# Four attention layers on one core: transfers queued by expected readiness, VectorE in source order, and the later weights' casts on POOL

## The chip, the core and the metric

The kernel runs on one core of a Trainium2 chip. The metric is the device time of one execution in microseconds. The engines are PE (matrix products), ACT (ScalarE), DVE (VectorE), POOL (GpSimd) and SP, whose queue issues all transfers of this kernel. Each engine takes its instructions strictly in the order of its own queue; an instruction whose operand is not there holds everything behind it on that engine.

## The reference

```python
# x: 2048 x 512, 32 heads of 16; layers A, B, A, B, each with wqkv (512 x 1536) and wo (512 x 512)
def layer(x, wqkv, wo, window):
    h = (x - mean(x)) / sqrt(var(x) + 1e-5)
    q, k, v = heads(h @ wqkv)
    scores = q @ k.T * 16 ** -0.5
    if window:                       # layers A: 0 <= query - key < 256
        scores = where(mask, scores, -1e9)
    return x + merge(softmax(scores) @ v) @ wo
```

Layers 0 and 2 are windowed (A), layers 1 and 3 are full (B).

## The kernel before, in words

Rows are handled in four chunks of 512 and heads in eight groups of four ("qd"). For a chunk and a group the attention makes transposed scores (keys on partitions, 512 queries free) in PSUM on PE (L673), ACT takes the exponential of two heads at a time out of PSUM (L677, tile `e`), in windowed layers POOL zeroes the edges of the window in `e` (L739 and L742), and PE multiplies `e` with the values, to which a column of ones is joined, into an accumulator `acc` (L717 full, L749 windowed), two steps later than the scores. Score banks come from a PSUM pool with three buffers; two accumulators stay. A full layer has 16 steps of two exponentials for each group, a windowed layer three steps.

Between the steps "side work" is issued: the output product of the chunk before (`wo`), the normalisation and transposes of the next layer (`T`), its keys, queries and values, and in layer 0 the preparation of weights that are needed later. A small planner in Python sets the order: a running clock in microseconds, `clock[0]`, is advanced by assumed costs, and each work has a time at which it is ready. A step of a windowed layer takes at least 2.4 units of that clock, a step of a full layer at least 1.8. PE takes its instructions in this source order (`manual_schedule`). For the other engines and for SP a scheduler chooses the order when the program is built, from priorities in source order and its own idea of when operands will be there; `high_priority` moves the copy `oe` ahead.

Steps that the change touches:

- `epilogue` (L609 to L650), at the end of a group: DVE copies the accumulator to `oe` (L617); SP sends its sums to `lt` (L622) and all of it to scratch DRAM `scr` (L623). After each second group `reciprocals` reads `lt`, takes reciprocals on DVE (L630 to L633), sends them to DRAM as `rcp` (L635), and loads `o` (L640) and the broadcast reciprocals `r` (L641). `normalised` multiplies `o` by `r` on DVE (L644) and splits the result into two f16 parts `oh` (L646, L647). `late` holds the two steps back by 4.5 and 8 units of the clock.
- `project` (L456): twelve f16 products make a bank of keys or queries (L387); the first part goes out through ACT (L479) or, in full layers, DVE (L481), the remainder through DVE (L482), the squares through ACT (L485) or POOL (L487), and SP stores both parts (L492 to L496). `queries` and `key_shift` add a row `m`.
- `wo` (L575) and `wo_part` (L592): DVE scales the output product to `dx` (L586, L604), adds it to `x` (L587, L605), SP stores `x` (L588, L606), and `stats` and `norm` (L402 to L417) prepare the next layer's normalised rows `xh`.
- `prep` (L338) prepares five of the eight weights during layer 0: `maxima` (L284) takes the largest absolute value over the four row blocks in one DVE instruction, `scales` makes scales from it, and `parts` (L319) multiplies by them on POOL (L326), casts to f16 on DVE (L332) and takes the remainder on POOL (L333).
- `load_full` (L686) and `load_win` (L698) load the next group's queries `qt` (two buffers) and keys `kt` (three buffers) a group ahead; `weights` (L367) loads a prepared weight into one of two buffers.

Of the kernel before, what the change touches and what calls it, by code (L numbers as in the profile page):

```python
# [19 lines left out]
P = 128  # L20
# [168 lines left out]
def fast_path(ctx, tc, flag, a_x, a_wqkv, a_wo, b_wqkv, b_wo, out):  # L189
# [12 lines left out]
    ctx.enter_context(tc.manual_schedule(engines={mybir.EngineType.PE}))  # L202
# [5 lines left out]
    CM, DN, WT, ST, LN, pend = {}, {}, {}, {}, {}, []  # L208

    clock, DONE, ONR = [0.0], {}, {}  # L210

    def spent(us):
        clock[0] += us
        return us
# [60 lines left out]
    def maxima(ty, s, raw, ahead):  # L275

        n = f"{ty}_{s}"
        if s == 3:
            for k in range(NC):
                nc.vector.tensor_scalar(raw[:, k, :], raw[:, k, :], upv[:, ty, k:k + 1], None, op0=ALU.mult)  # L280
        cm = CM[ty, s] = vp.tile([P, NHT], F32, name=f"wc{n}", tag="wc", bufs=8)
        if ahead:
            am = vp.tile([P, D], F32, name=f"wa{n}", tag="o")
            nc.vector.tensor_reduce(am, raw.rearrange("p k f -> p f k"), axis=AX.X, op=ALU.max,  # L284
                                    apply_absolute_value=True)
            yield
            pt = bank(f"wt{n}").rearrange("p (t f) -> p t f", f=P)
            for t in range(NHT):
                nc.tensor.transpose(pt[:, t, :], am[:, t * P:(t + 1) * P], ident)
            nc.vector.tensor_reduce(cm, pt, axis=AX.X, op=ALU.max)  # L290
            return
        for t in range(NHT):
            pt = bank(f"wt{n}_{t}")
            for k in range(NC):
                nc.tensor.transpose(pt[:, k * P:(k + 1) * P], raw[:, k, t * P:(t + 1) * P], ident)
            nc.vector.tensor_reduce(cm[:, t:t + 1], pt, axis=AX.X, op=ALU.max, apply_absolute_value=True)

    def scales(ty, s):

        n = f"{ty}_{s}"  # L300
        cm = CM.pop((ty, s))
# [4 lines left out]
        for v, name in ((up, "u"), (dn, "d"))[0 if s == 3 else 1:]:  # L306
            dg = vp.tile([P, NHT, P], F32, name=f"{name}g{n}", tag="oe")
            nc.vector.tensor_tensor(dg, ident[:, None, :].broadcast_to([P, NHT, P]),
                                    v[:, :, None].broadcast_to([P, NHT, P]), ALU.mult)
            yield  # L310
            pb = bank(f"{name}b{n}")
            nc.tensor.matmul(pb, onesf, dg.rearrange("p t f -> p (t f)"), start=True, stop=True)
            if name == "u":
                nc.vector.tensor_copy(gcol[ty], pb)
            else:
                DN[ty, s] = vp.tile([P, D], F32, name=f"wd{n}", tag="dn", bufs=2)
                nc.scalar.activation(DN[ty, s], pb, AF.Copy)

    def parts(ty, s, raw, act):  # L319

        dnb = DN.pop((ty, s))
        w = wp.tile([P, NC, 2, D], F16, name=f"w{ty}_{s}", tag="vf", bufs=NQ)
        for k in range(NC + 1):
            if k < NC:
                r = raw[:, k, :]
                (nc.vector if act else nc.gpsimd).tensor_tensor(r, r, dnb, ALU.mult)  # L326
            if k:
                r, (hi, lo) = raw[:, k - 1, :], (w[:, k - 1, b, :] for b in range(2))
                if act:
                    nc.scalar.activation(hi, r, AF.Copy)  # L330
                else:
                    nc.vector.tensor_copy(hi, r)  # L332
# [34 lines left out]
    def weights(ty, s, n, t=None):  # L367

        w = wp.tile([P, NC, 2, D], F16, name=f"w{n}", tag="w", bufs=WB)
        if t is None:  # L370
            nc.sync.dma_start(w, wd[ty, s])
            return w
        nc.sync.dma_start(w[:, :, :, :P], wd[ty, s][:, :, :, t * P:(t + 1) * P])
# [46 lines left out]
    def load_x(l, c):  # L420
        xs = []
        for i in range(4):
            k = 4 * c + i
            x = vp.tile([P, D], F32, name=f"x{l}_{k}", tag="x", bufs=XB)
            nc.sync.dma_start(x, a_x[0, k * P:(k + 1) * P, :] if l == 0 else xd[k])
            xs.append(x)
# [29 lines left out]
    def project(l, s, c, act, w=None, ht=None):  # L456
# [3 lines left out]
        if not w:  # L460
            w = weights(ty, s, n, ht)
            yield wait(8)
        xc = XC[l, c]
# [7 lines left out]
        for t in range(NHT) if ht is None else (ht,):  # L471
# [3 lines left out]
            settle(not sqs)  # L475
            sp = vp.tile([P, 2, QC], F16, name=f"sp{n}_{t}", tag="sp", bufs=3)
# [7 lines left out]
            if act:  # L484
                nc.scalar.activation(sq, ps, AF.Square, scale=e)  # L485
# [4 lines left out]
            d = dst[8 * t:8 * t + 8].rearrange("h (d b) n -> (h d) b n", b=4)  # L490
            if s:
# [30 lines left out]
    def queries(l, c, act, w=None, ht=None):  # L522
        sqs = yield from project(l, 0, c, act, w, ht)

        def rest():
            ph = squares(f"q{l}_{c}_{ht}", sqs)

            m = vp.tile([P, QC], F16, name=f"m{l}_{c}_{ht}", tag="m", bufs=1)
# [7 lines left out]
            for t in sqs:  # L536
                nc.sync.dma_start(rows(qs[l % 2, c])[8 * t:8 * t + 8, 3, :], m[32 * t:32 * t + 8, :])
# [6 lines left out]
    def key_shift(l, ht=None):  # L544
# [4 lines left out]
        nc.vector.tensor_reduce(kx[r], KM[l][r], axis=AX.X, op=ALU.max)  # L549
        m = vp.tile([P, QC], F16, name=f"mk{l}_{ht}", tag="m", bufs=1)  # L550
        nc.vector.tensor_scalar(m[r], ones[r], kx[r], -0.515, op0=ALU.mult, op1=ALU.mult)
        for t in range(NHT) if ht is None else (ht,):
            nc.sync.dma_start(rows(kf)[8 * t:8 * t + 8, 7, :].rearrange("h (c n) -> h c n", n=QC),
                              m[32 * t:32 * t + 8, None, :].broadcast_to([8, NQ, QC]))

    def values(l, c, act, w=None):
        n = f"{l}_{c}"
        if not w:
            w = weights(l % 2, 2, f"v{n}")
            yield wait(8)  # L560
        xc = XC[l, c]
# [13 lines left out]
    def wo(l, c):  # L575

        w = weights(l % 2, 3, f"o{l}_{c}")
        yield wait(8)

        xs = load_x(l, c)  # L580
        for i in range(4):
# [5 lines left out]
            nc.vector.tensor_add(xs[i], xs[i], d)  # L587
            nc.sync.dma_start(xd[k], xs[i])  # L588
            stats(l + 1, c, i, xs[i])
            yield -MM if PH["full"] else -12 * MM  # L590

    def wo_part(c, t):  # L592
# [6 lines left out]
        for i in range(4):  # L599
# [5 lines left out]
            nc.vector.tensor_add(xs[i], xs[i], d)  # L605
            nc.sync.dma_start(out[0, k * P:(k + 1) * P, :] if t == NHT - 1 else xd[k], xs[i])  # L606
            yield -MM

    def epilogue(l, c, qd, a, act):  # L609
        n = f"{l}_{c}_{qd}"  # L610
        t, u = divmod(qd, 2)
        oe = vp.tile([P, QC], F32, name=f"oe{n}", tag="oe")
# [5 lines left out]
        if u == 0:  # L618
            EP["scr"] = dp.tile([8, 32, QC], F32, name=f"scr{n}", tag="scr", bufs=4)
            EP["lt"] = vp.tile([P, 32], F32, name=f"lt{n}", tag="lt")  # L620
        scr, lt = EP["scr"], EP["lt"]
        nc.sync.dma_start(lt[64 * u:64 * u + 64, :], oe[DH:P:32, :].rearrange("c (b n) -> c b n", n=32))  # L622
        nc.sync.dma_start(scr[4 * u:4 * u + 4], oe)  # L623
# [3 lines left out]
        def reciprocals():  # L627

            d = vp.tile([P, 2], F32, name=f"d{n}", tag="d")
# [5 lines left out]
            nc.sync.dma_start(rcp.rearrange("h (b n) -> h b n", n=32), lt)  # L635
# [3 lines left out]
            r = vp.tile([P, QC], F32, name=f"r{n}", tag="r", bufs=1)  # L639
            nc.sync.dma_start(o, scr[:, :DH, :])  # L640
            nc.sync.dma_start(r, rcp[:, None, :].broadcast_to([8, DH, QC]))  # L641

            def normalised():
                nc.vector.tensor_tensor(o, o, r, ALU.mult)  # L644
# [4 lines left out]
            late.append((clock[0] + 8, normalised))  # L649
        late.append((clock[0] + 4.5, reciprocals))  # L650
# [35 lines left out]
    def load_full(l, c, qd):  # L686
# [3 lines left out]
        nc.sync.dma_start(qt, qs[1, c][pair].rearrange("r p n -> p r n"))  # L690
# [7 lines left out]
    def load_win(l, c, qd):  # L698
# [4 lines left out]
        nc.sync.dma_start(qt, qs[0, c][pair].rearrange("r p n -> p r n"))  # L703
        nc.sync.dma_start(kt[:, :, WIN:WIN + QC], kw[c][pair].rearrange("r p n -> p r n"))
        if c:
            nc.sync.dma_start(kt[:, :, :WIN], kw[c - 1][pair, :, QC - WIN:].rearrange("r p n -> p r n"))
        return kt, qt

    def attn_full(l, c, qd, kt, qt, a):
        for j in range(NT):  # L710
            es_ = []
# [14 lines left out]
    def attn_win(l, c, qd, kt, qt, a):  # L726
        first = True
# [236 lines left out]
    def NN(c, after=()):  # L964
        def gen():
            xs = load_x(0, c)
            yield wait(12 if c > 1 else 0)
            for i in range(4):
                stats(0, c, i, xs[i])
# [14 lines left out]
    for i in range(4):  # L984
        stats(0, 0, i, xs[i])
# [81 lines left out]

    okay = cp.tile([P, 2], F32, name="okay")
# [34 lines left out]
```

## Time and profile before

| | us |
|---|---|
| median of the runs (3) | 2992.46 (2990.77 to 3002.14) |
| profiled execution | 2998.08 |
| its span | 2996.4 |
| PE busy | 2757.5 (92%) |
| ACT busy | 2402.0 (80%) |
| DVE busy | 895.1 (30%) |
| POOL busy | 557.5 (19%) |

The busy shares are means over stages with different limits: layer 0 reaches to about 605 us, layer 1 to 1585, layer 2 to 2040, layer 3 to the end. A row of the profile names the line, the engine, the operation, what it writes and reads, and the shape. In a timeline the bracket at the end of a row is the time that the engine stood idle before it, and what released it.

### The profile page before, as it was taken

The numbers are of one execution on the slowest core, as the hardware profiler recorded it, in microseconds if no ns is written. First come the engines' busy times: TensorE is split into PE (matmuls) and PEld (weight loads), VectorE is DVE, ScalarE is ACT, GpSimd is POOL, SyncE is SP. The second block draws the span as 40 slices with busy tenths as digits, with TensorE's granted clock in tenths as the row PEclk, the third lists the DMA queues.
The fourth block names the chain that finished last, engine by engine and source line by source line (L and its number), as shares of the span: only waits on it lengthen the run. The fifth ranks groups of instructions, "written<-read, shape, count | busy, mean of one in ns | idle before, by whom it ended". The sixth has DMA issues, their size and how long they took to land.

```text
span 2996.4 us, 51979 instructions
## 1 busy us (share of the span) xinstructions
PE 2757.5 (92%) x20314; PEld 751.0 (25%) x20314; DVE 895.1 (30%) x1866; ACT 2402.0 (80%) x2703; POOL 557.5 (19%) x1127
## 2 busy tenths in 40 slices
PE   6787898899999999999999888789999999999996
PEld 3233333321122112212222333331211221112111
DVE  7665544401112113111212545531221222122212
ACT  3454555389999999999997666429999999999996
POOL 2546554100000000000002566500000000000000
PEclk8899999999999999999999999889999999999998
DMA  6575675532223232222323656432343333433332
GB/s 223 194 240 195 208 226 178 171 108 97 77 87 102 94 104 93 96 84 88 108 88 124 211 188 184 147 117 84 123 128 127 120 120 128 129 121 121 119 113 68
DMA packets 291408, 399.34 MB, mean 133 GB/s; under 512 B 70352, under 2 KB 173264, under 8 KB 283856
## 3 DMA queue, kind: packets, MB, share of 16 engines
q1 hardware_dynamic: 291152, 395.92, 40.6%
q8 instruction: 161, 2.64, 0.4%
q14 instruction: 95, 0.78, 0.1%
HBM read 263.19 MB, written 131.60 MB: 132 GB/s over the span
## 4 chain that ended last, share of the span: by engine, by line
PE 65%; ACT 10%; DVE 9%; DMA 9%; issue 4%; POOL 2%; SPq 1%; ACTq 0%; DVEq 0%; POOLq 0%
PE acc L717 25%; PE s L673 18%; PE acc L387 9%; ACT e L677 9%; PE pq L387 4%; PE pv L387 4%; DMA r<-rcp 4%; DMA rcp<-lt 3%; PE po L387 2%; PE acc L749 2%; DVE xh L417 1%; DMA scr<-oe 1%; DVE o L644 1%; DVE xh L414 1%; DVE xn L414 1%
## 5 line engine op out<-in xcount | busy, mean ns | idle before, releaser
L677 ACT ACTIVATE e<-s 128x1024 f32<-128x1024 f32 (+2 forms) x2432 | 2244.8, 1109 | 184.1 <-PE s L673 179.2
L717 PE MATMUL acc<-e,vt 128*17 128x512 f32 x8192 | 1078.6, 598 | 3.1 <-DVE oe L617 3.0
L673 PE MATMUL s<-qt,kt 64*128 64x512 f16 (+3 forms) x5504 | 798.7, 357 | 83.7 <-ACT e L677 14.2
L673 PEld LDWEIGHTS <-kt 64*128 64x128 f16 x5504 | 218.9, 94 | 944.9 <-issue 915.6
L742 POOL TENSOR_SCALAR_AFFINE_SELECT e<-e 128x256 f32<-128x256 f32 x512 | 223.7, 444 | 209.1 <-ACT e L677 208.4
L617 DVE COPY oe<-acc 128x512 f32<-128x512 f32 x128 | 88.1, 688 | 516.2 <-PE acc L717 461.9
L647 POOL TENSOR_TENSOR oh<-o,oh 128x512 f16<-128x512 f32 x32 | 37.1, 1159 | 1079.8 <-DVE oh L646 1079.8
L717 PEld LDWEIGHTS acc<-e,vt 128*17 128x17 f32 x8192 | 136.4, 95 | 351.1 <-issue 323.9
L739 POOL TENSOR_SCALAR_AFFINE_SELECT e<-e 128x256 f32<-128x256 f32 x448 | 194.3, 439 | 143.1 <-ACT e L677 140.6
L387 PE MATMUL pq<-xc,w 128*128 128x512 f16 x816 | 198.3, 397 | 12.6 <-ACT e L677 5.6
L749 PE MATMUL acc<-e,vt 128*17 128x384 f32 (+2 forms) x2816 | 204.3, 400 | 1.3 <-POOL e L739 1.1
L387 PEld LDWEIGHTS <-w 128*128 128x128 f16 x1152 | 106.2, 100 | 250.3 <-issue 157.8
L644 DVE TENSOR_TENSOR o<-o,r 128x512 f32<-128x512 f32 x64 | 53.2, 832 | 368.2 <-DMA r<-rcp 368.0
L387 PE MATMUL po<-wo,oh 128*128 128x512 f16 x444 | 113.9, 413 | 46.0 <-DVE dx L586 29.3
L479 ACT ACTIVATE sp<-pq,es 128x512 f16<-128x512 f32 x68 | 46.7, 687 | 108.6 <-PE pq L387 82.6
L387 PE MATMUL pv<-wv,xc 128*128 128x512 f16 x576 | 131.8, 385 | 1.5 <-ACT sq L485 0.6
L487 POOL TENSOR_TENSOR sq<-sp 128x512 bf16<-128x512 f16 x28 | 29.1, 1039 | 558.9 <-DVE sp L481 558.9
L387 PEld LDWEIGHTS <-oh 128*128 128x128 f16 x768 | 69.2, 101 | 213.3 <-issue 138.8
L570 ACT ACTIVATE vt<-pv 128x512 f32<-128x512 f32 x52 | 31.1, 597 | 110.1 <-PE pv L387 110.1
L387 PEld LDWEIGHTS <-xc 128*128 128x128 f16 x768 | 70.5, 99 | 140.7 <-issue 70.0
L481 DVE TENSOR_SCALAR sp<-acc,es 128x512 f16<-128x512 f32 x28 | 21.0, 750 | 268.2 <-PE acc L387 247.8
L387 PE MATMUL acc<-xc,w 128*128 128x512 f16 x336 | 95.4, 386 | 3.7 <-DVE sp L482 3.7
(128 smaller groups left out, 1486.3 us busy)
## 6 DMA issues: line engine op xcount, KB each, us to landing
kt<-kf SPq DMA_DIRECT2D x128, 512.0 KB
qt<-qs SPq DMA_DIRECT2D x128, 256.0 KB
scr<-oe SPq DMA_DIRECT2D x128, 256.0 KB
xd<-x SPq DMA_DIRECT2D x96, 256.0 KB
x<-xd SPq DMA_DIRECT2D x96, 256.0 KB
w<-wd SPq DMA_DIRECT2D x22, 1024.0 KB
kt<-kw SPq DMA_DIRECT2D x64, 256.0 KB
o<-scr SPq DMA_DIRECT2D x64, 256.0 KB
```

The lines of the kernel that those rows point to most:

```text
L387: nc.tensor.matmul(ps, a, b, start=(i == 0), stop=(i == len(pairs) - 1))
L414: norm1 = lambda o: nc.vector.tensor_scalar(o, xs[i], mv[:, i, 0:1], y[:, i:i + 1], op0=ALU.subtract, op1=ALU.mult)
L479: nc.scalar.activation(sp[:, 0], ps, AF.Copy, scale=e)
L617: nc.vector.tensor_copy(oe, a)
L644: nc.vector.tensor_tensor(o, o, r, ALU.mult)
L647: (nc.gpsimd if l % 2 else nc.vector).tensor_tensor(ohl[:, 1], o, ohl[:, 0], ALU.subtract)
L673: nc.tensor.matmul(ps[:, h, s0:s0 + wd_], kt[R * h:R * h + R, pr, kc:kc + P], qt[R * h:R * h + R, pr, qc:qc + wd_], start=True, stop=True)
L677: nc.scalar.activation(e[:, :, w0:w1], ps[:, :, w0:w1], AF.Exp, scale=SCALE)
L717: nc.tensor.matmul(a[32 * h:32 * h + DH + 1, :], V[l, j // 4][:, j % 4, 4 * qd + h, :], es_[h // 2][:, h % 2, :], start=(j == 0), stop=(j ...
L739: nc.gpsimd.affine_select(v, v, pattern=[[0, 2], [-1, P]], compare_op=ALU.is_gt, fill=0.0, base=0, channel_multiplier=1)
L742: nc.gpsimd.affine_select(v, v, pattern=[[0, 2], [1, P]], compare_op=ALU.is_ge, fill=0.0, base=0, channel_multiplier=-1)
L749: nc.tensor.matmul(a[32 * h:32 * h + DH + 1, q * P:(q + nb) * P], V[l, (4 * c + j) // 4][:, j % 4, 4 * qd + h, :], es_[h // 2][:, h % 2, s ...
```

## The change

1. SP and DVE join PE in `manual_schedule`: both take their instructions in source order. The priority of `oe` has no more effect on DVE.
2. Most transfers are no longer written into the source where their data is made. `post` puts them on a list with an expected time (`clock[0]` plus a delay); `run_posts`, called whenever the clock advances, issues those whose time has come, in order of these times. `need` issues at once what a following step reads; `number` counts the uses of a buffer tag and issues the posts that read a buffer which is about to be taken again.
3. The delays of `late` become 5 and 9. The load of `r` is posted 4 units after the reciprocals. The second half of a full group's keys is posted 18 units after instead of 1, when the group follows its neighbour.
4. Weights prepared for later: the f16 cast moves from DVE to POOL, the maximum is taken in two halves with a pause between, its tile uses another buffer tag, and pauses of 8 or 6 units become 4.
5. ACT's square reads the stored f16 part in SBUF instead of the product in PSUM. For queries the order of the two stores is exchanged.

```diff
-    ctx.enter_context(tc.manual_schedule(engines={mybir.EngineType.PE}))
+    ctx.enter_context(tc.manual_schedule(engines={mybir.EngineType.PE, mybir.EngineType.SP, mybir.EngineType.DVE}))
...
+    posts, made, serial = [], {}, [0]
+    def post(out_, in_, delay, dst=None, of=None):
+        serial[0] += 1
+        posts.append((clock[0] + delay, serial[0], out_, in_, dst, of))
+        run_posts()
+    def run_posts(test=lambda x: False):
+        go = sorted(x[:2] for x in posts if x[0] <= clock[0] or test(x))
+        by = {x[:2]: x for x in posts}
+        for k in go:
+            x = by[k]
+            posts.remove(x)
+            nc.sync.dma_start(x[2], x[3])
+    def need(*dst):
+        run_posts(lambda x: x[4] in dst)
+    def number(tag, bufs):
+        made[tag] = made.get(tag, 0) + 1
+        run_posts(lambda x: x[5] is not None and x[5][0] == tag and x[5][1] <= made[tag] - bufs)
+        return tag, made[tag]
     def spent(us):
         clock[0] += us
+        run_posts()
         return us
...
         if ahead:
-            am = vp.tile([P, D], F32, name=f"wa{n}", tag="o")
-            nc.vector.tensor_reduce(am, raw.rearrange("p k f -> p f k"), axis=AX.X, op=ALU.max,
-                                    apply_absolute_value=True)
-            yield
+            am = vp.tile([P, D], F32, name=f"wa{n}", tag="dn", bufs=2)
+            for h in range(2):
+                f = slice(h * D // 2, (h + 1) * D // 2)
+                nc.vector.tensor_reduce(am[:, f], raw[:, :, f].rearrange("p k f -> p f k"), axis=AX.X, op=ALU.max,
+                                        apply_absolute_value=True)
+                yield
...
                 if act:
                     nc.scalar.activation(hi, r, AF.Copy)
                 else:
-                    nc.vector.tensor_copy(hi, r)
+                    nc.gpsimd.tensor_copy(hi, r)
...
         for _ in maxima(ty, s, raw, True):
-            yield wait(8 if s == 3 else 6)
+            yield wait(4)
...
-            nc.sync.dma_start(w, wd[ty, s])
-            return w
+            post(w, wd[ty, s], 1.5, ("w", n))
...
             if act:
-                nc.scalar.activation(sq, ps, AF.Square, scale=e)
+                nc.scalar.activation(sq, sp[:, 0], AF.Square)
...
             if s:
-                nc.sync.dma_start(d[:, 0:2], sp[:, 0:1].broadcast_to([P, 2, QC]))
-                nc.sync.dma_start(d[:, 2], sp[:, 1])
+                post(d[:, 0:2], sp[:, 0:1].broadcast_to([P, 2, QC]), 2.5, where, of)
+                post(d[:, 2], sp[:, 1], 3.5, where, of)
             else:
-                nc.sync.dma_start(d[:, 0:2], sp)
-                nc.sync.dma_start(d[:, 2], sp[:, 0])
+                post(d[:, 2], sp[:, 0], 2.5, where, of)
+                post(d[:, 0:2], sp, 3.5, where, of)
...
-            nc.vector.tensor_add(xs[i], xs[i], d)
-            nc.sync.dma_start(xd[k], xs[i])
-            stats(l + 1, c, i, xs[i])
+            x, of = xs[i]
+            nc.vector.tensor_add(x, x, d)
+            post(xd[k], x, 3.0, ("xd", k), of)
+            stats(l + 1, c, i, x)
...
-        nc.sync.dma_start(lt[64 * u:64 * u + 64, :], oe[DH:P:32, :].rearrange("c (b n) -> c b n", n=32))
-        nc.sync.dma_start(scr[4 * u:4 * u + 4], oe)
+        post(lt[64 * u:64 * u + 64, :], oe[DH:P:32, :].rearrange("c (b n) -> c b n", n=32), 2.0, ("lt", l, c, t), of)
+        post(scr[4 * u:4 * u + 4], oe, 2.0, ("scr", l, c, t), of)
...
         def reciprocals():
+            need(("lt", l, c, t))
...
-            nc.sync.dma_start(rcp.rearrange("h (b n) -> h b n", n=32), lt)
+            post(rcp.rearrange("h (b n) -> h b n", n=32), lt, 1.5, ("rcp", l, c, t), of_lt)
...
+            need(("scr", l, c, t))
             nc.sync.dma_start(o, scr[:, :DH, :])
-            nc.sync.dma_start(r, rcp[:, None, :].broadcast_to([8, DH, QC]))
+            post(r, rcp[:, None, :].broadcast_to([8, DH, QC]), 4.0, ("r", l, c, t))
             def normalised():
+                need(("rcp", l, c, t))
+                need(("r", l, c, t))
                 nc.vector.tensor_tensor(o, o, r, ALU.mult)
...
-            late.append((clock[0] + 8, normalised))
-        late.append((clock[0] + 4.5, reciprocals))
+            late.append((clock[0] + 9, normalised))
+        late.append((clock[0] + 5, reciprocals))
...
-        nc.sync.dma_start(qt, qs[1, c][pair].rearrange("r p n -> p r n"))
+        need(("qs", 1, c), ("kf",))
+        early = KL.get("n") == (l, c, qd - 1)
+        KL["n"] = (l, c, qd)
+        post(qt, qs[1, c][pair].rearrange("r p n -> p r n"), 1.0, ("qt", n))
...
-            nc.sync.dma_start(kt, kf[pair, :, v * S // 2:(v + 1) * S // 2].rearrange("r p n -> p r n"))
+            post(kt, kf[pair, :, v * S // 2:(v + 1) * S // 2].rearrange("r p n -> p r n"),
+                 1.0 + 17 * v * early, ("kt", n, v))
```

The remaining lines of the diff do the same to the other transfers: the window's loads, the row `m` (2.5 and 1.5), `wo_part` (2.5) and the weights by quarter (1.5); `need` stands ahead of the steps that read them, and what is left is issued at the end.

More of the change, by code (lines that the diff above doesn't have):

```diff
@@ L462, in project @@
             yield wait(8)
+            need(("w", n))
         xc = XC[l, c]
@@ L536, in rest @@
             for t in sqs:
-                nc.sync.dma_start(rows(qs[l % 2, c])[8 * t:8 * t + 8, 3, :], m[32 * t:32 * t + 8, :])
+                post(rows(qs[l % 2, c])[8 * t:8 * t + 8, 3, :], m[32 * t:32 * t + 8, :], 2.5, ("qs", l % 2, c), of)
         pend.append((clock[0] + 3.6, rest))
@@ L552, in key_shift @@
         for t in range(NHT) if ht is None else (ht,):
-            nc.sync.dma_start(rows(kf)[8 * t:8 * t + 8, 7, :].rearrange("h (c n) -> h c n", n=QC),
-                              m[32 * t:32 * t + 8, None, :].broadcast_to([8, NQ, QC]))
+            post(rows(kf)[8 * t:8 * t + 8, 7, :].rearrange("h (c n) -> h c n", n=QC),
+                 m[32 * t:32 * t + 8, None, :].broadcast_to([8, NQ, QC]), 1.5, ("kf",), of)
     def values(l, c, act, w=None):
@@ L560, in values @@
             yield wait(8)
+            need(("w", f"v{n}"))
         xc = XC[l, c]
@@ L578, in wo @@
         yield wait(8)
+        need(("w", f"o{l}_{c}"))
         xs = load_x(l, c)
@@ L604, in wo_part @@
             nc.vector.tensor_tensor(d, ps, gcol[1], ALU.mult)
-            nc.vector.tensor_add(xs[i], xs[i], d)
-            nc.sync.dma_start(out[0, k * P:(k + 1) * P, :] if t == NHT - 1 else xd[k], xs[i])
+            x, of = xs[i]
+            nc.vector.tensor_add(x, x, d)
+            post(out[0, k * P:(k + 1) * P, :] if t == NHT - 1 else xd[k], x, 2.5, ("xd", k), of)
             yield -MM
@@ L702, in load_win @@
         pair = slice(2 * qd, 2 * qd + 2)
-        nc.sync.dma_start(qt, qs[0, c][pair].rearrange("r p n -> p r n"))
-        nc.sync.dma_start(kt[:, :, WIN:WIN + QC], kw[c][pair].rearrange("r p n -> p r n"))
+        need(("qs", 0, c), ("kw", c), ("kw", c - 1))
+        post(qt, qs[0, c][pair].rearrange("r p n -> p r n"), 1.0, ("qt", n))
+        post(kt[:, :, WIN:WIN + QC], kw[c][pair].rearrange("r p n -> p r n"), 1.0, ("kt", n))
         if c:
-            nc.sync.dma_start(kt[:, :, :WIN], kw[c - 1][pair, :, QC - WIN:].rearrange("r p n -> p r n"))
+            post(kt[:, :, :WIN], kw[c - 1][pair, :, QC - WIN:].rearrange("r p n -> p r n"), 1.0, ("kt", n))
         return kt, qt
     def attn_full(l, c, qd, kt, qt, a):
+        need(("qt", f"{l}_{c}_{qd}"))
         for j in range(NT):
+            if j % 8 == 0:
+                need(("kt", f"{l}_{c}_{qd}", j // 8))
             es_ = []
@@ L726, in attn_win @@
     def attn_win(l, c, qd, kt, qt, a):
-        first = True
+        need(("qt", f"{l}_{c}_{qd}"), ("kt", f"{l}_{c}_{qd}"))
         for u, tiles in enumerate(WTILES):
```

23 lines of the change are left out of this document (17 added, 6 removed).

## The prediction

> **What bounds the kernel now.** I read the forty slices first, then busy time by stage. The four rows of stages below are columns of core, start:end, length, then busy time of PE, its weight loads, DVE, ACT and POOL with their counts, granted clock, DMA share, GB/s.
>
> ```profile
> PE   6787898899999999999999888789999999999996
> ACT  3454555389999999999997666429999999999996
> PEclk8899999999999999999999999889999999999998
> ...
> 75.00:605.00 530.00, 445.69 (x3504) 186.99 (x3503) 276.97 (x556) 264.24 (x347) 248.82 (x528) 0.94 0.63 202
> 1585.00:2040.00 455.00, 386.54 (x3321) 149.06 (x3319) 193.03 (x436) 263.75 (x321) 196.28 (x487) 0.92 0.51 159
> 605.00:1585.00 980.00, 954.20 (x6764) 202.73 (x6763) 166.73 (x373) 928.33 (x1003) 46.46 (x43) 1.00 0.28 93
> 2040.00:2970.00 930.00, 915.85 (x6507) 185.14 (x6499) 194.96 (x358) 920.99 (x997) 45.41 (x42) 1.00 0.37 118
> ```
>
> Four stages carry the span. The full layers (605 to 1585 and 2040 to 2970) are ACT's: it is idle 51.7 us in the first and 9.0 us in the second, so VectorE or queue order can win little there. The windowed layers (75 to 605 and 1585 to 2040) are nobody's: PE is idle 84.3 + 68.5 = 152.8 us at a granted clock of 0.94 and 0.92, with DVE, ACT and POOL half free. What the change can win lies in PE's gaps there, so I listed those of 0.9 us or more and followed each to what released it. Two families hold most of them.
>
> **Casts out of VectorE, and the maximum in halves.**
>
> ```profile
> L332 DVE CAST w<-wr x20: 403/1424/1504, 121.1 to 367.7; 128x512 f16<-128x512 f32 x20
> ...
> L332 DVE CAST w<-wr 128x512 f16<-128x512 f32 x20 | 26.8, 1369 | 14.1 <-POOL wr L326 14.1
> ...
> L284 DVE TENSOR_REDUCE wa<-wr x5: 3611/3682/3698, 73.3 to 332.6; 128x512 f32<-128x2048 f32 x5
> ```
> ```profile
> 125.88 0.40 PE L673 MATMUL s<-qt,kt 64*128 64x256 f16 x2 [3.70 <-DVE km L519]
> ...
> 142.20 0.44 PE L673 MATMUL s<-qt,kt 64*128 64x384 f16 x2 [3.71 <-ACT sq L485]
> 212.01 1.09 PE L289 MATMUL wt<-ident,wa 128*128 128x128 f32 x4 [5.51 <-DVE wa L284]
> 214.59 4.14 PE L387 MATMUL pq<-xc,w 128*128 128x512 f16 x12
> ...
> 240.44 4.84 PE L387 MATMUL po<-wo,oh 128*128 128x512 f16 x12 [6.39 <-DVE dx L586]
> 251.58 4.40 PE L387 MATMUL po<-wo,oh 128*128 128x512 f16 x12 [4.77 <-DVE dx L586]
> ...
> 367.81 4.31 PE L387 MATMUL po<-wo,oh 128*128 128x512 f16 x12 [5.47 <-DVE dx L586]
> ...
> 451.41 2.76 PE L387 MATMUL pv<-wv,xc 128*128 128x512 f16 x12
> ```
>
> A cast takes 0.40 us at best and 1.42 us in the median, with POOL at work beside it (mean 1.37), and for 14.1 us VectorE stands at casts whose POOL multiplication is not done. Just ahead of each of the five gaps of 3.70, 3.71, 6.39, 4.77 and 5.47 us (24.0 us in all) VectorE is in such casts, and the reduction, output product or projection that frees PE's bank stands behind them. After the change all 20 casts are POOL's. I take three quarters as won, 18.0 us, because some of what stood behind the casts is late for a second reason. The 5.51 us gap is a maximum of 3.68 us that began late; its half takes 1.84 us, and its PE transposes wait only for a half that starts at once: 5.51 - 1.84 = 3.7 us.
>
> The price is on POOL. No row shows this copy there, so I bound it:
>
> ```profile
> L326 POOL TENSOR_TENSOR wr<-wr,wd 128x512 f32<-128x512 f32 x20 | 26.9, 1364 | 1.2 <-ACT wd L317 1.2
> ...
> L245 POOL MEMSET ones<- 128x512 f16 x1 | 0.5, 524 | 0.0
> ```
>
> Writing 512 f16 without reading took 0.52 us; a two-input operation over 512 f32 took 1.36 us. The copy is one input between them: 0.9 us, 20 of them 18 us (10 to 27). POOL is busy 249 of 530 us, and its selects feed PE two steps later, so I charge a third: 6 us. Below nothing it cannot go: on POOL it only adds.
>
> A row speaks against this edit:
>
> ```profile
> 1872.76 7.05 DVE L644 TENSOR_TENSOR o<-o,r 128x512 f32<-128x512 f32 x1 [3.71 <-DMA r<-rcp]
> ```
>
> In the midst of POOL selects a VectorE product took 7.05 us (0.69 in the row at 1893.00 below). So a longer POOL run can stop VectorE too. The Trainium skill, "SBUF — State Buffer", Who interferes with whom, says that GpSimd shares a port pair with VectorE under an exclusive lock and that the second to come is blocked for the whole instruction; the cast's 0.40 against 1.42 us and this row agree. By that rule a moved copy still holds VectorE for about its own 0.9 us: of 20 x 1.37 + 14.1 = 41.5 us freed, 18 would return, the 18.0 us above would be 10.2, and the time 7.8 us longer than my sum gives.
>
> **The order of VectorE and of the queue.** The normalising product of a pair of groups waits for its reciprocals to come back from DRAM:
>
> ```profile
> DVE o L644 <- DMA r<-rcp: 59.3, 14, 7.9
> ...
> DVE o L644 <- DMA r<-rcp: 74.5, 16, 9.4
> ...
> DVE o L644 <- DMA r<-rcp: 102.8, 15, 11.3
> ```
> ```profile
> 1884.16 0.35 DVE L633 RECIPROCAL lt<-lt 128x32 f32<-128x32 f32 x1
> ...
> 1893.00 0.69 DVE L644 TENSOR_TENSOR o<-o,r 128x512 f32<-128x512 f32 x1 [6.27 <-DMA r<-rcp]
> ```
> ```profile
> 380.03 4.13 PE L387 MATMUL pq<-xc,w 128*128 128x512 f16 x12 [2.15 <-DVE dx L586]
> 480.91 4.08 PE L387 MATMUL po<-wo,oh 128*128 128x512 f16 x12 [4.07 <-DVE dx L586]
> 1653.22 0.39 PE L673 MATMUL s<-qt,kt 64*128 64x256 f16 x4 [4.00 <-DVE dx L586]
> 1894.35 5.28 PE L387 MATMUL po<-wo,oh 128*128 128x512 f16 x12 [7.85 <-DVE dx L586]
> 1926.85 4.44 PE L387 MATMUL pq_h<-xc,w_h 128*128 128x512 f16 x12 [2.86 <-DVE xc L450]
> ```
> ```profile
> 1001.43 3.77 ACT L677 ACTIVATE e<-s 128x1024 f32<-128x1024 f32 x4 [2.35 <-PE s L673]
> 1061.48 4.82 ACT L677 ACTIVATE e<-s 128x1024 f32<-128x1024 f32 x5 [2.28 <-PE s L673]
> 1319.38 1.94 ACT L677 ACTIVATE e<-s 128x1024 f32<-128x1024 f32 x2 [3.81 <-PE s L673]
> ```
>
> The three sums are the first windowed layer, the second, and the first full one. VectorE stands 59.3 + 74.5 = 133.8 us at 30 products, 4.5 us each, with output products and copies out of PSUM queued behind. The product began 8.8 us after the reciprocal began, of which 6.27 us was waiting: it came to the head of the queue some 2.6 us after. In the changed source it is emitted 9 units of the source's clock after the reciprocals, and its place in the source is its place in the queue. Its load is posted 4 units after, instead of holding SP until the reciprocals have landed. A full layer's step is 1.8 units and at least two exponentials of about 1.1 us, so 9 units are about 11 us there, more than the 8.8 us needed. PE gaps 2.15 + 4.07 + 4.00 + 7.85 + 2.86 = 20.9 us and three ACT gaps of 8.4 us in the full layer come from this wait: 29.4 us, of which I take two thirds, 19.6 us, since in the windowed layers the margin is thinner.
>
> Each long PE gap has a second cost. Twelve matmuls take 2.76 us when warm, but 4.14, 4.84, 4.40, 4.31, 4.13, 4.08, 5.28 and 4.44 us after these gaps: 13.5 us too much, two thirds of it won, 9.0 us.
>
> Against that stand the costs of a fixed order.
>
> ```profile
> PEld acc L717 <- DVE oe L617: 24.6, 54, 1.8
> ...
> DVE sp L482 <- ACT sp L479: 84.9, 35, 4.8
> ```
>
> The copy `oe` loses its priority. In the full layers one accumulator serves all, and PE waits for 54 of 64 copies, 0.46 us each. One more 0.69 us instruction ahead of each is 44 us of PE time; two more score buffers hide most from ACT, so I charge a fifth: 8.8 us (0 to 44). The second half of a projection follows in the source at once, while ACT makes its first half: 35 waits of 2.4 us now. If all 73 wait, 92 us more stand in VectorE; PE's part of such standing is 20.9 / 133.8 above, so 14 us; half of it, 7 us, because ACT also gets freer, as follows.
>
> ```profile
> ACT sq L485 <- DVE sp L482: 38.1, 29, 5.1
> ...
> PE s L673 <- ACT sq L485: 9.5, 8, 3.7
> ```
>
> The square now reads the SBUF copy. The bank no longer passes through DVE to ACT, 29 waits of ACT go, and the PE waits for squares, 9.5 us less the 3.71 counted above, halve: 3 us.
>
> With SP in source order the key loads are held back:
>
> ```profile
> SPq L690 <- PE s L673: 229.4, 48, 15.7
> ```
>
> SP stands 229 us before query loads whose buffer is in use, with everything behind it late. I give the cure nothing beyond the 19.6 us: ACT in the full layers hides it. If that cover failed, a late key tile would show as ACT idle, which the bounds carry. The prologue and the tail keep their chains, at nothing: their steps are released by the same PE results in source order.
>
> **Sum.** 18.0 + 3.7 + 19.6 + 9.0 + 3 - 6 - 8.8 - 7 = 31.5 us won. The profiled execution took 2998.08 us (span 2996.4 and 1.7 around it), 5.6 above the median 2992.46. It becomes 2966.6, and on the median 2961.0 us.
>
> **Rivals.** Bigger gain: all of the gaps go and the fixed order costs nothing, 24.0 + 3.7 + 29.4 + 13.5 + 6 = 76.6, less 6: about 2922 us. For it speaks that the gaps have few causes; against it, that 153 us of PE idle has many small pieces.
>
> One wait for another, or the posts do not do what they say, because demands flush them at once: the r waits stay. Without the 19.6 us and the 4.6 us of clock that follow them it is 31.5 - 24.2 = 7.3 won: 2985 us. For it: transfers in these layers share busy DMA queues (0.63 and 0.51).
>
> POOL locks VectorE: a prepared weight is four pieces of 1.36 + 0.9 + 1.36 us on POOL (the subtraction taken like the multiplication), 14.5 us that no cast interrupts any more. If it stops VectorE for half, 7.2 us, in five preparations, 36 us are lost and neither the casts' gain nor a separate 6 us counts: 36 + 8.8 + 7 - 19.6 - 4.6 - 3 = 24.6 us slower, 3017 us. It decides from 2.3 us per preparation. For it speaks the 7.05 us row; against it, that in the present bursts casts did get through at 1.4 us each. This is the rule of the port lock at its worst.
>
> **How the numbers follow.** About 0.5% (15 us) separates a change from none. Forecast 0.50; its own range is 2925 to 2987, from most of the won terms to half of them less all costs (53.3 / 2 - 21.8 = 4.9 us won), and 0.05 of it ends within 0.5%. Bigger gain 0.15. Exchange of waits 0.15, of which 0.05 ends over 15 us faster. POOL lock 0.20. Faster 0.45 + 0.15 + 0.05 = 0.65, same 0.05 + 0.10 = 0.15, slower 0.20. The range 2905 to 3015 leaves out a third of the bigger gain (0.05) and over half of the lock (0.12).
>
> **What would show it.** Right: no VectorE cast from `wr`; waits of the product for `r` in the windowed layers well under 133.8 us; both windowed stages together some 20 us shorter, at a clock above 0.94 and 0.92; full layers within 10 us. Wrong: VectorE products of several us beside POOL runs; ACT idle above 52 and 9 us in the full layers; PE gaps released by `oe` or `sp`.

## The result and the profile after

The changed kernel took 3012.8 us (median; 3004.6 to 3016.2) against 2994.57 for the kernel before beside it: a ratio of 1.0055, 95% interval 1.0038 to 1.0073, so 18 us slower. The forecast was 2961.0, faster. The profiled execution took 3004.58 us (span 3002.9), the fastest one of the changed kernel; its trace therefore shows a smaller loss (6.5 us of span) than the medians (18.2 us).

These are the two slices and the busy times by stage of the changed kernel, columns as before:

```profile
PE   6686999899999999999999789889999999999996
...
PEclk8898999999999999999999899989999999999998
```
```profile
75.00:610.00 535.00, 445.67 (x3487) 184.52 (x3486) 287.80 (x569) 261.10 (x343) 263.22 (x548) 0.92 0.62 206
610.00:1590.00 980.00, 960.02 (x6793) 205.19 (x6795) 170.30 (x377) 931.28 (x1009) 46.52 (x43) 1.00 0.28 95
1590.00:2045.00 455.00, 394.60 (x3350) 149.51 (x3346) 197.12 (x438) 266.88 (x326) 200.12 (x487) 0.92 0.50 161
2045.00:2973.00 928.00, 909.98 (x6482) 183.03 (x6474) 193.66 (x356) 918.62 (x993) 44.43 (x41) 1.00 0.36 118
```

The first windowed stage is 5 us longer for the same work of PE, at a clock of 0.92 instead of 0.94. The full stages have ACT idle 48.7 and 9.4 us (51.7 and 9.0 before). These windows end at round times and do not hold quite the same work. From the first to the last output copy `oe` of a layer the windowed layers take 453.3 and 316.6 us (447.6 and 317.4 before) and the full ones 953.6 and 924.8 (962.9 and 923.2 before); the first copy comes 5.8 us later, and the step from layer 0 to layer 1 takes 107.5 us instead of 103.9. So the first full layer won 9.3 us, and in this trace the loss lies ahead of the first copy, in layer 0 and at its end. The waits of VectorE in the windowed stages (first stage, then the second):

```profile
DVE sp L518 <- ACT sp L515: 78.5, 29, 7.8
...
DVE o L693 <- DMA r<-rcp: 9.5, 5, 4.4
...
DVE sp L518 <- ACT sp L515: 26.8, 8, 5.2
DVE sp_h L518 <- ACT sp_h L515: 22.6, 4, 10.4
DVE o L693 <- DMA r<-rcp: 22.3, 7, 8.2
```

The waits for `r` fell from 133.8 to 31.8 us, as forecast. But PE has a wait that is not in the list of before:

```profile
PE s L722 <- DMA kt<-kw: 20.0, 5, 5.7
...
PE s L722 <- DMA kt<-kw: 14.5, 6, 7.5
PE po L419 <- DMA wo<-wd: 4.7, 2, 2.6
```

Scores wait 34.5 us for keys of the window. The timeline of PE and that of SP's queue show how one of these gaps arises; the third fence is SP's queue in the kernel before, at the same place.

```profile
1691.79 0.22 PE L722 MATMUL s<-qt,kt 64*128 64x128 f16 x1
...
1700.28 1.03 PE L722 MATMUL s<-qt,kt 64*128 64x128 f16 x8 [7.50 <-DMA kt<-kw]
```
```profile
1688.28 0.37 SPq L228 DMA_DIRECT2D rcp<-lt  x1
1691.93 0.62 SPq L228 DMA_DIRECT2D r<-rcp  x1
1692.60 0.96 SPq L228 DMA_DIRECT2D kw<-sp  x2
1693.66 0.58 SPq L228 DMA_DIRECT2D lt<-oe  x1
1694.30 0.49 SPq L228 DMA_DIRECT2D scr<-oe  x1
1694.88 0.39 SPq L228 DMA_DIRECT2D qt<-qs  x1
1695.31 1.02 SPq L228 DMA_DIRECT2D kt<-kw  x2
```
```profile
1676.55 0.59 SPq L622 DMA_DIRECT2D lt<-oe  x1
1677.19 0.45 SPq L623 DMA_DIRECT2D scr<-oe  x1
...
1680.88 0.37 SPq L635 DMA_DIRECT2D rcp<-lt  x1
1681.35 0.41 SPq L703 DMA_DIRECT2D qt<-qs  x1
1681.81 0.46 SPq L704 DMA_DIRECT2D kt<-kw  x1
1682.32 0.47 SPq L706 DMA_DIRECT2D kt<-kw  x1
...
1685.60 0.62 SPq L641 DMA_DIRECT2D r<-rcp  x1
```

This is the border between two chunks. The source writes a chunk's first loads only when the chunk begins. The scheduler of before took them out of that order and issued them ahead of `r`. In source order they stand behind `r`, two stores of keys and two stores of `oe`, are issued at 1695.3, and PE starts 5 us later.

### The profile page after: what moved, and what is told of

The parts are those of the page before. It is cut to its first block, busy times and chain, and to the rows that moved or that the text cites. A ratio compares the mean times of both kernels' runs of the same rounds, so it can differ in the third digit from the quotient of the medians.

```text
span 3002.9 us, 52009 instructions
## 1 busy us (share of the span) xinstructions
PE 2762.0 (92%) x20314; PEld 747.9 (25%) x20314; DVE 901.6 (30%) x1851; ACT 2401.0 (80%) x2703; POOL 574.0 (19%) x1147
## 4 chain that ended last, share of the span: by engine, by line
PE 69%; ACT 8%; DVE 8%; DMA 6%; issue 3%; POOL 2%; SPq 1%; ACTq 0%; DVEq 0%; POOLq 0%
PE acc L775 26%; PE s L722 18%; PE acc L419 9%; ACT e L726 8%; PE pq L419 4%; PE pv L419 4%; PE acc L807 3%; PE po L419 3%; DMA kt<-kf 2%; SPq L228 1%; DMA kt<-kw 1%; DMA rcp<-lt 1%; DMA wo<-wd 1%; DVE xn L446 1%; DVE xh L449 1%
## 5 line engine op out<-in xcount | busy, mean ns | idle before, releaser
L722 PE MATMUL s<-qt,kt 64*128 64x512 f16 (+3 forms) x5504 | 793.9, 357 | 99.9 <-DMA kt<-kw 34.5
L800 POOL TENSOR_SCALAR_AFFINE_SELECT e<-e 128x256 f32<-128x256 f32 x512 | 232.4, 460 | 193.0 <-ACT e L726 192.0
L797 POOL TENSOR_SCALAR_AFFINE_SELECT e<-e 128x256 f32<-128x256 f32 x448 | 196.5, 444 | 142.0 <-ACT e L726 140.1
L807 PE MATMUL acc<-e,vt 128*17 128x384 f32 (+2 forms) x2816 | 214.2, 407 | 4.4 <-POOL e L797 4.2
L419 PE MATMUL po<-wo,oh 128*128 128x512 f16 x444 | 107.6, 397 | 31.2 <-DMA wo<-wd 21.1
L481 ACT ACTIVATE xc<-pt 128x512 f16<-128x512 f16 x52 | 30.6, 602 | 84.6 <-PE pt L478 84.2
```

The lines of the kernel that those rows point to most:

```text
L419: nc.tensor.matmul(ps, a, b, start=(i == 0), stop=(i == len(pairs) - 1))
L722: nc.tensor.matmul(ps[:, h, s0:s0 + wd_], kt[R * h:R * h + R, pr, kc:kc + P], qt[R * h:R * h + R, pr, qc:qc + wd_], start=True, stop=True)
L797: nc.gpsimd.affine_select(v, v, pattern=[[0, 2], [-1, P]], compare_op=ALU.is_gt, fill=0.0, base=0, channel_multiplier=1)
L800: nc.gpsimd.affine_select(v, v, pattern=[[0, 2], [1, P]], compare_op=ALU.is_ge, fill=0.0, base=0, channel_multiplier=-1)
L807: nc.tensor.matmul(a[32 * h:32 * h + DH + 1, q * P:(q + nb) * P], V[l, (4 * c + j) // 4][:, j % 4, 4 * qd + h, :], es_[h // 2][:, h % 2, s ...
```

## The experiments

"Changed" means the changed kernel. The kernels ran as three sets, each on a chip of its own together with the kernel before (2993.93, 2994.55 and 2993.67 us there); a ratio is against the kernel before of the same set. The first set holds the three kernels of the first question and the casts alone on the kernel before; the second VectorE's order alone, the casts on VectorE and on ACT with SP free, and the early loads in the changed kernel; the third the rest. A difference between kernels of two sets also holds the difference between two chips, which for the kernel before is under 1 us.

**Which order costs?** Three kernels differ from the changed one in the set of engines held to source order.

```diff
-    ctx.enter_context(tc.manual_schedule(engines={mybir.EngineType.PE, mybir.EngineType.SP, mybir.EngineType.DVE}))
+    ... engines={PE, DVE}      # e1_sp_free
+    ... engines={PE, SP}       # e2_dve_free
+    ... engines={PE}           # e3_both_free
```

> The changed kernel with SP's order left to the scheduler again (VectorE stays in source order). Theory A (SP in source order issues a chunk's first key load only when the chunk begins): PE's waits for that load, 34.5 us over the two windowed layers in the changed kernel, fall under 10 us, and the time falls by some 20 us against the changed kernel, to about 2990. Theory B (the loss is POOL holding VectorE): VectorE instructions of several us beside POOL stay, PE's gaps of 9.09 and 7.81 us stay, the time moves by less than 6 us.

Measured 2968.58 us, ratio 0.9909 [0.9890, 0.9927]: 44 us faster than the changed kernel. PE's waits for `kt` fall from 34.5 to 0.6 us. The 44 us are twice the 20 expected. Between output copies the kernel is 13.4 us shorter in layer 0, 4.7 at the step to layer 1 and 22.6 in layer 2, and under 2 us shorter in each of the full layers.

> The changed kernel with VectorE's order left to the scheduler again (SP stays in source order). If VectorE's source order is what costs (theory C): over 10 us faster than the changed kernel. If the source order is a gain, as the prediction had it: VectorE's waits for the reciprocals' load, 31.8 us in the windowed layers of the changed kernel, go back towards the 133.8 us of the kernel before, and it is 10 to 25 us slower than the changed kernel. Theory A says nothing on it: the load waits of 34.5 us stay.

Measured 3024.34 us, 1.0087 [1.0069, 1.0104]: 11.5 us slower than the changed kernel. VectorE's waits for `r` in the windowed layers go from 31.8 to 79.2 us, and the waits for `kt` stay (39.5 us).

> The changed kernel with SP and VectorE both left to the scheduler: what remains is the casts on POOL, the halves, the square and the delays. Theory A: no late key loads (under 10 us of PE waits), about 2990. Theory B: the gaps beside POOL's runs stay, and it is still 5 to 20 us slower than the kernel before.

Measured 2998.94 us, 1.0018 [1.0006, 1.0030]. The waits for `r` in the two windowed stages of this kernel are nearly what they were before (59.3 and 74.5):

```profile
DVE o L693 <- DMA r<-rcp: 57.3, 13, 10.6
...
DVE o L693 <- DMA r<-rcp: 70.3, 14, 9.1
```

So VectorE's source order wins 30.4 us (2998.94 to 2968.58) and SP's loses 44.2 us with it and 25.4 us without it. With SP in source order VectorE's wins 11.5 us. With both freed the late key loads are gone (0.8 us), as theory A had it, and the kernel is 5.0 us slower than the kernel before, the least that theory B had.

**VectorE's order alone, on the kernel before.**

```diff
-    ... engines={PE}
+    ... engines={PE, DVE}
...
-            am = vp.tile([P, D], F32, name=f"wa{n}", tag="o")
+            am = vp.tile([P, D], F32, name=f"wa{n}", tag="dn", bufs=2)
```

> The kernel before with VectorE in source order and nothing else (the maximum's tile takes another buffer tag, which that order needs; SP stays with the scheduler, casts on VectorE, delays 4.5 and 8). If the order alone brings the gain: waits for the reciprocals' load in the windowed layers fall from 133.8 us to under 70, and it is 5 to 20 us faster than the kernel before. If it needs the longer delays and the freed casts: waits stay above 90 us, and it is 0 to 20 us slower.

Measured 2972.66 us, 0.9930 [0.9913, 0.9948]: 21.9 us won by two lines, and the waits for `r` in the windowed layers are 42.2 us. Between output copies layer 0 is 5.1 us shorter than before, layer 1 9.8 and layer 2 18.4, and the first copy comes 9.2 us later. No run here has this order without the other tag.

**The casts.** First alone on the kernel before; then the reverse, VectorE and ACT in POOL's place, on the kernel with SP free.

```diff
# e4_casts, on the kernel before
-                    nc.vector.tensor_copy(hi, r)
+                    nc.gpsimd.tensor_copy(hi, r)
# e6_dve_casts and e7_act_casts, on e1_sp_free
-                    nc.gpsimd.tensor_copy(hi, r)
+                    nc.vector.tensor_copy(hi, r)       # e6
+                    nc.scalar.activation(hi, r, AF.Copy)   # e7
```

> The kernel before with one line changed: the f16 cast of the later weights on POOL. Prediction's step: 10 to 18 us faster than before, less 6. Theory B: VectorE instructions stretch to several us beside POOL's unbroken run, five preparations lose 2 to 7 us each, and it is 0 to 25 us slower than before.

Measured 2984.5 us, 0.9964 [0.9948, 0.9981]: 9.4 us won. Between 75 and 610 us PE's waits for `dx` fall from 22.9 to 5.3 us, but those for POOL's selects, which now stand behind the casts, rise from 0.8 us to this:

```profile
PE acc L749 <- POOL e L739: 19.6, 12, 8.1
```

> The version with SP left to the scheduler and VectorE in source order (2968.6 us), with the later weights' casts back on VectorE. Prediction's step: the casts held VectorE, so 10 to 20 us slower than that version. Theory B (a POOL copy holds VectorE about as long as the cast did): within 6 us of it.

Measured 2954.2 us, 0.9866 [0.9847, 0.9884]: back on VectorE the casts win 14.4 us over the same kernel with POOL's.

> The same version (2968.6 us) with the later weights' casts on ACT instead of POOL. Theory B (POOL's unbroken runs hold VectorE and PE behind it): VectorE instructions beside the preparation shorten, and it is 5 to 15 us faster than that version. Rival: 20 copies of about 0.63 us push ACT's exponentials back in layer 0, and it is 0 to 10 us slower.

Measured 2962.51 us, 0.9894 [0.9877, 0.9912]: 6.1 us less than with POOL's casts and 8.3 more than with VectorE's. Its interval overlaps both, so neither difference is shown.

The same move wins 9.4 us on the kernel before and loses 14.4 on the changed source with VectorE in source order. The groups of casts (with SP free and the casts on VectorE, then the changed kernel) show that the cast itself is cheap on either engine; the third fence is VectorE of the changed kernel while POOL prepares weights, and the fourth PE behind it.

```profile
L364 DVE CAST w<-wr 128x512 f16<-128x512 f32 x20 | 15.6, 806 | 2.7 <-POOL wr L358 2.7
```
```profile
L364 POOL CAST w<-wr 128x512 f16<-128x512 f32 x20 | 11.9, 606 | 0.0
```
```profile
129.30 1.06 DVE L44 TENSOR_SCALAR v<-mv 128x4 f32<-128x4 f32 x1
130.39 1.19 DVE L45 TENSOR_SCALAR y<-v 128x4 int32<-128x4 int32 x1
131.61 0.52 DVE L46 TENSOR_SCALAR y<-y 128x4 int32<-128x4 int32 x1
132.16 1.18 DVE L48 TENSOR_TENSOR z<-y,v 128x4 f32<-128x4 f32 x1
...
138.48 0.16 DVE L49 SCALAR_TENSOR_TENSOR z<-z,y 128x4 f32<-128x4 f32 x1
...
273.24 9.06 DVE L693 TENSOR_TENSOR o<-o,r 128x512 f32<-128x512 f32 x1 [0.96 <-DMA r<-rcp]
```
```profile
139.59 0.62 PE L541 MATMUL phk_None<-sq,hsum 128*32 128x512 bf16 x4 [7.81 <-DVE sp L518]
...
285.37 4.68 PE L419 MATMUL po<-wo,oh 128*128 128x512 f16 x12 [9.09 <-DVE m_None L573]
```

An operation of four elements takes 0.52 to 1.19 us instead of 0.16, and one product 9.06 us. The two operations at 131.61 and 132.16 end within 0.02 us of the POOL instruction that began just ahead of them:

```profile
131.50 0.61 POOL L364 CAST w<-wr 128x512 f16<-128x512 f32 x1
132.07 1.26 POOL L358 TENSOR_TENSOR wr<-wr,wd 128x512 f32<-128x512 f32 x1
```

The same comes with SP free and POOL's casts (first fence: VectorE), and less of it with the casts back on VectorE (second fence: PE at the place of the first gap above):

```profile
269.73 7.83 DVE L693 TENSOR_TENSOR o<-o,r 128x512 f32<-128x512 f32 x1 [6.41 <-DMA r<-rcp]
```
```profile
136.48 0.62 PE L541 MATMUL phk_None<-sq,hsum 128*32 128x512 bf16 x4 [4.17 <-DVE sp L518]
```

In that last kernel no VectorE instruction between 75 and 610 us takes over 2.2 us. What POOL of the changed kernel did during the 9.06 us, the first and the last of thirteen instructions that began in them:

```profile
273.45 0.60 POOL L364 CAST w<-wr 128x512 f16<-128x512 f32 x1
...
281.83 1.47 POOL L365 TENSOR_TENSOR w<-wr,w 128x512 f16<-128x512 f32 x1
```

The Trainium skill, "SBUF — State Buffer", Who interferes with whom, says that a VectorE instruction with two inputs in SBUF contends with a GpSimd instruction that reads SBUF. The 9.06 us row agrees, but a wait over one instruction would be 1.3 us; here it lasts over a run of them. That a cast on VectorE breaks this run, since POOL's remainder must wait for it, is argued and not shown. With the casts on ACT the remainder must wait as well, and there the product takes 3.54 us, but small operations still take 1.07 to 1.25 us and PE has a gap of 7.82 us.

VectorE is not the whole of the 14.4 us: PE's waits for POOL's selects, between 75 and 610 us, are 5.2 us with SP free and POOL's casts and 0.6 with VectorE's. Nor is VectorE's order alone shown to turn the sign. With both engines free a product takes 12.71 us, and that kernel, which also has the halves, the square and the delays, takes 14.4 us more than the kernel with the casts alone. It was not run with VectorE's casts.

**The late first loads.** The changed kernel, with the first group of the next windowed chunk loaded during the last group of a chunk, as soon as its queries and keys are made.

```diff
+        ahead = {}
...
-                ops = load(l, c, qds[0])
+                ops = ahead.pop(c, None) or load(l, c, qds[0])
...
                             settle(False)
+                            if (qd == qds[-1] and c + 1 < NQ and c + 1 not in ahead and not pend and
+                                    ("K", l, c + 1) in DONE and ("Q", l, c + 1) in DONE):
+                                ahead[c + 1] = load(l, c + 1, qds[0])
```

> The changed kernel (SP and VectorE in source order) with one addition: the loads of a windowed chunk's first group are written into the source during the last group of the chunk before, as soon as that chunk's keys and queries are issued. Theory A (the cost of SP's source order is these first loads): PE's waits for key loads fall from 34.5 us to under 10, and it takes 2980 to 2990 us, 23 to 33 less than the changed kernel. Rival (source order makes many transfers late, not these alone): under 15 us faster than the changed kernel.

Measured 2988.03 us, 0.9976 [0.9965, 0.9987]: 24.8 us faster than the changed kernel. The waits for `kt` fall to 10.0 and 2.6 us.

**Are the losses separate?** The casts back on VectorE in the changed kernel, without and with the early loads.

> The changed kernel with the casts of later weights back on VectorE (SP and VectorE in source order). If the casts on POOL and SP's order are two separate losses, the 14.4 us that the casts brought with SP free come here too: 3012.8 - 14.4 = 2998 us. If SP's order holds the same steps late that the POOL run holds late, the gain is smaller: 3007 us or more. VectorE products beside the preparation's POOL work take 1 to 2 us again, not 9.

Measured 2997.98 us, 1.0018 [1.0005, 1.0030]: 14.8 us won, as with SP free (14.4). No product of `o` and `r` in layer 0 takes over 0.9 us.

> As the kernel before this one, and a windowed chunk's first loads stand in the source during the last group of the chunk before. If all three are separate: 2988.0 - 14.4 = 2973.6 us, so 19.4 us behind the same kernel with SP free (2954.2), which is then what SP's order still costs. If the late first loads are the whole of it once the casts are on VectorE, it comes within 5 us of 2954.

Measured 2976.1 us, 0.9941 [0.9928, 0.9955]: 21.9 us more won, and 21.9 us left to the same kernel with SP free. Its waits of PE in the windowed stages:

```profile
PE s L722 <- DMA kt<-kw: 10.8, 2, 5.8
...
PE po L419 <- DMA wo<-wd: 2.5, 1, 2.5
...
PE po L419 <- DMA wo<-wd: 5.8, 3, 2.5
...
PE s L722 <- DMA kt<-kw: 4.7, 3, 2.9
```

With SP free there is one wait of 7.7 us for `qt` in place of these keys, and one of 2.4 for `wo`. The rows so name about 14 of the 21.9 us (15.5 - 7.7, and 8.3 - 2.4). The rest lies in small pieces. By output copies 9 us of the whole fall in layer 2, some 5 between the last group of layer 0 and the first of layer 1, and 4 in layer 0. I have not settled it.

**Halves and square.** On the kernel with SP free and VectorE's casts.

```diff
             for h in range(2):
-                f = slice(h * D // 2, (h + 1) * D // 2)
-                nc.vector.tensor_reduce(am[:, f], raw[:, :, f]...)
+                if h == 0:
+                    nc.vector.tensor_reduce(am, raw...)
                 yield
...
-                nc.scalar.activation(sq, sp[:, 0], AF.Square)
+                nc.scalar.activation(sq, ps, AF.Square, scale=e)
```

> The best kernel so far with the maximum of a later weight whole again (one instruction of 3.66 us in place of two of 1.92, the pauses kept) and ACT's square reading the product in PSUM. The prediction gave these two edits 3.7 + 3 = 6.7 us, so 2961 us. If in source order neither is on the path that sets the end, 2954 us. Waits of PE for squares come back (9.5 us in the kernel before).

Measured 2966.99 us, 0.9915 [0.9903, 0.9928]: 12.8 us lost. PE's waits for squares in layer 0 are back:

```profile
PE phk_None L541 <- ACT sq L521: 11.2, 3, 8.3
...
PE s L722 <- ACT sq L521: 5.7, 3, 3.2
```

They do not explain the 12.8 us: in the kernel with the two edits PE waits 18.3 us for `sp` instead, and that wait is gone here. Layer 0 is 8.0 us longer between its output copies and the first copy 2.8 us later. Which of the two edits wins how much is open.

**The prologue.** On the same kernel, the first two normalised rows ahead of the first weight's pieces.

```diff
     run(scales(0, 1))
+    first = [norm(0, 0, i) for i in range(2)]
     run(parts(0, 1, raw[1], True))
...
-    run(transpose(0, 0, True))
+    run(transpose(0, 0, True, first))     # takes the two rows from first
```

> The best kernel so far (VectorE in source order, SP free, casts on VectorE) with the first two normalised rows of layer 0 written into the source ahead of the first weight's four pieces. In the kernel before the scheduler made them while VectorE waited for that weight, and the first keys started 31.12 us after the start against 33.99. If this is where the prologue lost, the first output copy comes 3 to 6 us earlier than its 101.7 and the time is 2949 to 2951 us. If the later weights' maxima are what comes late, nothing moves: 2954 us.

Measured 2948.71 us, 0.9847 [0.9831, 0.9862]. The first output copies of three kernels (before; SP free and VectorE's casts; this one):

```profile
95.11 0.69 DVE L617 COPY oe<-acc 128x512 f32<-128x512 f32 x1 [0.46 <-PE acc L749]
```
```profile
101.74 0.68 DVE L661 COPY oe<-acc 128x512 f32<-128x512 f32 x1
```
```profile
101.49 0.68 DVE L662 COPY oe<-acc 128x512 f32<-128x512 f32 x1
```

The expected 3 to 6 us at the first copy did not come; only 0.25 did. The kernel is the fastest of all, 45 us below the kernel before, but its interval overlaps that of the kernel without this edit, so the edit itself is not shown to win.

## Why the prediction was wrong

The single steps between the two kernels, each a difference of medians above (the second compares the order alone with the kernel that has the maximum whole and the square from PSUM, and holds the posts, delays and pauses that are left when SP is free; the intervals of those two overlap, so this step is not shown to win):

| step | from, to | us |
|---|---|---|
| VectorE in source order | 2994.55, 2972.66 | -21.9 |
| posts, delays, pauses | 2972.66, 2966.99 | -5.7 |
| maxima in halves, square from SBUF | 2966.99, 2954.2 | -12.8 |
| casts to POOL | 2954.2, 2968.58 | +14.4 |
| SP in source order | 2968.58, 3012.8 | +44.2 |
| sum | | +18.2 |

Taken in another order the steps would share the time out otherwise, as the 44.2 and 25.4 us of SP show.

- **SP's queue: the step that failed.** "With SP in source order the key loads are held back: ... I give the cure nothing beyond the 19.6 us: ACT in the full layers hides it." I read SP's row as time that a better order could only release, and looked for the danger in the full layers, where ACT does hide it. The order is paid for in the windowed layers, which I had myself named nobody's: nothing hides a late load there, and the source writes a chunk's first loads late. Its term in the sum was nothing; measured, it costs 44.2 us, of which loads written earlier recover 21.9 to 24.8. What the other 19 to 22 us are is open beyond the rows above.
- **Casts.** 18.0 - 6 = 12 us was won in the sum. On the kernel before 9.4 came, but the nearness is partly luck: POOL's price, charged at 6, shows there as 18.8 us more of PE's waits for the selects, and PE's waits for `dx`, `km` and `sq` fell by 25.4 us. I had added the term to a new order of VectorE without asking whether it holds there, and in that arrangement it loses 14.4. The rival of the port lock was to decide from 2.3 us per preparation; 14.4 / 5 = 2.9, if all of it were the lock. I had counted the row of 7.05 us as agreeing with that rule, but it is not a wait over one instruction: POOL ran selects of 0.40 us there, one behind the other. The rival's time of 3017 is near the measured 3012.8, but not for its reason: without SP's order the kernel with POOL's casts is still 25 us faster than before.
- **Waits for `r`.** Right, and the largest gain. 19.6 + 4.6 of clock, less 8.8 and 7 for the fixed order, is 8.4 us; measured 21.9, with the delays of before, so the longer delays are not needed for it. The 8.8 us for `oe` were too high: PE waits 24.4 us for these copies in the changed kernel and 24.6 before, and the first full layer is 9.3 us shorter. The 7 us for `sp` were not: VectorE's waits grew from 57.9 + 19.0 + 11.9 to 78.5 + 26.8 + 22.6 us, and in the first windowed stage PE now waits 18.4 us for `sp`, where it waited 13.1 for the squares behind it. PE gaps released by `sp` were one of the signs of being wrong, and a VectorE product of several us beside POOL runs was another; both came.
- **Clock.** The 9.0 us did not come in the changed kernel: granted 0.92 and 0.92. New gaps took the place of the old.
- **Halves and square.** 3.7 + 3 = 6.7 us; measured 12.8 together, on another order. The direction was right, the size about half, and the waits for squares that the 3 us stood for mostly became waits for `sp`.
- **Prologue.** "At nothing" was wrong by 5.8 us at the first output copy (95.11 to 100.91). With VectorE and SP left to the scheduler it is 97.25, and with VectorE alone left to it 97.53, so most of it is VectorE's order. The normalised rows are not its cause: in the last experiment the first keys start at 31.29 us, as before (31.12), and the copy is still at 101.49. The cause is open.

## What to carry to other kernels

When a queue is taken from a scheduler and fixed to source order, list for every stage the instructions that the scheduler had issued ahead of their place in the source, above all the first loads of each loop, and price each by the wait of the engine that is not covered in that stage. Fix one engine's order at a time: here VectorE's order alone was worth 22 us and the queue's order cost 44. A gain measured or argued in one arrangement of the work (the casts) need not keep its sign in another.

## What was not expected of the hardware

- Beside an unbroken run of POOL instructions VectorE operations over four elements took 0.52 to 1.19 us instead of 0.16, one after the other, and a product of 0.69 us took 9.06. In the kernel before a product took 7.05 us beside selects of 0.40 us.
- A 128x512 copy from f32 to f16 on POOL took 0.61 us, below the 0.9 us estimated from its neighbours; the same on VectorE took 0.81 us on average in source order and 1.37 before.
